# Query heads laid side by side by GpSimd ahead of the transposes, and a new order of loads, in a fused Sinkhorn-attention and token-mixing kernel

## The chip, the cores and the metric

The kernel runs on one core of a Trainium2 chip. The metric is the device time of one execution in microseconds (us). The kernel before takes 104.47 us (median of 4 runs, 104.46 to 104.66).

## What is computed

There are 4 batches with 8 heads, 768 positions and 64 columns per head; the positions form 8 blocks of 96.

```python
P = sort_net                                   # (4, 8, 8, 8)
for _ in range(5):                             # Sinkhorn
    P = exp(P - max(P, -1)); P /= sum(P, -1); P /= sum(P, -2)
k_s = einsum('bhij,bhjcd->bhicd', P, k_blocks); v_s = the same with v
attn = softmax(q_block @ k_s.T / 8) within each block
x = (attn @ v_s), heads side by side           # (4, 768, 512)
wq, wk = x @ w_q, x @ w_k                      # 64 columns each
out = relu((wq @ wk.T / 8) @ x) @ w_out        # (4, 768, 512), float32
```

The token mixing is reassociated: `wk.T @ x` is formed first (group G below), then multiplied by `wq`.

## The kernel before, in words

The whole program is written as one list of short items, `ORDER` (L18 to L42), and the loop at L479 issues them one by one. An item is a letter, a batch, a number and a last sign. Capital letters are groups of TensorE (PE) matmuls and the last sign is the PSUM bank; a small letter is the eviction of the group (q evicts Q, k evicts K, v evicts V, e is the exp of S, r and x evict P, and so on) and the last sign is the engine, A for ScalarE (ACT), D for VectorE (DVE), P for GpSimd (POOL), S for SyncE (SP). Each engine works through its items in the order of the list. Nothing is reordered later; waits come from the data and buffers that items share. `Q115` is thus the Q group of batch 1, number 1, into bank 5.

The groups on PE, for one batch:

- Q (L244, 3 groups): transposes of the query. The load leaves row p*6+r of a head in partition p, slot r. A group takes two slots r and four head pairs kp. For each it issues **two** transposes, one for each head (hh) of the pair: 64 columns of `Qn` as weights, the 128x128 identity `idb` as the moving operand, the result in one half of the 128 PSUM partitions. So a group has 16 matmuls and a batch 48. q evicts to `QT`.
- K (L266, 4 groups): the sorted key, with `M` (a Kronecker matrix of P, built by n, L223) as the moving operand; k evicts to `KT`. Each group writes two 64-partition halves.
- F and A for batch 0, V and the DMAs R (L316) for the others: the sorted value; it ends in `VT`.
- S (scores), P (attention times value, with a column for the sum), T (transposes of X), J (x times w_q and w_k), W, G, H and O (the last product, 4 matmuls of 512 columns each).
- Z: fillers at the start that compute nothing.

Tiles that matter here: `Qn`, `Kn`, `Vn` have three buffers each (L95, L96), one for a batch, and batch 3 goes into that of batch 0. `QT`, `KT`, `VT`, `E`, `X` have two. The first four heads of batch 0's query come by SP as float32 into a stage (L154) and are cast by ACT into `Qn` (items i04, i05, L185); the other four come with item l00.

All other loads are DMAs that POOL issues (u_l, L200): l*b*0 is the query of batch b, l*b*1 the key, l*b*2 the value, l03 w_q and w_k, l04 w_out. They convert from float32 to bfloat16 on their way and go through one queue (q0 in the profile). POOL's items in order:

```
l00 l01 l02 i00 i02 l03 l11 l10 l12 l04 n11 n10 l20 n21 n20
N11v l21 l30 N11v N10v N12v l22 l32 l31 n30 n31
```

The items N (u_N, L321) are **gates**: a copy of one element out of `Vs`, which POOL can only do once the eviction v of batch 1 with that number has written it. What stands behind a gate in POOL's list, such as the key of batch 2 (l21), is issued after it.

Of the kernel before, what the change touches and what calls it, by code (L numbers as in the profile page):

```python
# [9 lines left out]
BF16 = mybir.dt.bfloat16  # L10
# [5 lines left out]


ORDER = """  # L18
l00P l01P l02P i00P i02P l03P c00D c01D i01D Z080 l11P c02D i03A Z250 c03D Z350 i04A l10P c04D Z440
i05A Q027 c05D Q016 q02A Q005 Z540 q00A b00D l12P B004 Z020 q01A n01D n00D l04P K010 u00A n03D K002  # L20
n11P n02D k01A K036 k00D K024 k03A S020 n10P k02D S012 e02A S056 F034 e01A S000 f03D l20P e05A F022
A035 f02A S066 a03D e00A A024 F012 e06A a02D F000 f01A K136 n21P f00D P044 A013 r04D A002 k13D a01A
n20P K100 x04D S036 k10A a00D K114 e03A S040 k11D P002 e04A P016 r00D Q115 x00D r01D P020 x01D q11A
Q104 r02D P032 q10A x02D V116 T005 v11A N11v l21P l30P r03D Q124 x03D V100 t00A V126 q12A v10D T015
T033 T022 v12A N11v N10v N12v l22P t03D S110 l32P t02D t01A S123 V136 e11A J012 v13D J005 e12A J032
S150 R12S j01D J025 R15S e15A S106 j00D R10S Q214 R11S d01D l31P Q203 e10A R14S q21D R13S W002 Q225
q20D d00A S160 w00D W014 q22A K126 w01D G003 e16A n30P k12A G013 K230 g01D K224 n31P k23A S136 k22D
H002 e13A K200 h00D S244 k20A H026 h02A S200 K212 e20A k21D O057 e24A H010 o05D S212 O046 h01A S234
e21A O007 e23A O033 o00D o04A P140 S264 o03A y02S Q302 r14D e26A x14D P116 S144 r11D Q313 x11D e14A
P100 q30A P134 r10D x10D V206 q31A O022 r13D x13D v20A V230 T103 v23A P126 T135 t10A r12D V210 x12D  # L30
O014 o02A v21A y01S V222 t13D T117 o01D v22A T126 V330 t11D y00S V304 t12D R20S S252 v30A Q327 R21S
v33D R25S J106 e25A R24S q32D R22S J115 R23S J126 V310 j10A J135 S222 v31D j11A W104 V326 e22A d11S
W115 w10D K300 v32D d10A G104 k30A K322 R30S K336 R32S w11A S300 k32A R33S k33D G114 R31S e30A R35S
K312 g11D R34S S366 k31D S354 e36A H110 e35A H106 h11D S312 h10A S334 P210 e33A O107 r21D e31A x21D
P204 O116 o10A r20D x20D P230 o11A P222 r23D H124 y10S x23D T207 h12A O126 r22D x22D t20A P300 O145
o12A r30D x30D T214 o14A T227 P242 t21D S325 t22A S340 r24D O134 x24D e32A T237 e34A o13D P312 J205
t23A y11S r31D P330 x31D J214 J225 P326 r33D j20A x33D J234 T303 d20S j21A W202 O155 t30A r32D d21S
w20D x32D W212 G203 w21A o15D P340 T312 r34D G213 y12S x34D T327 t31D g21A T336 t32D H220 t33A H202
H214 h22D J307 J316 h21D J327 O251 j30A d30A W300 h20D J336 O247 w30A j31A o25D G300 d31A o24A W316
O221 y22S w31D G310 o22A O237 g31A H320 o23A H312 H304 h32A O206 y21S O217 o20A O351 o21A h30D h31A  # L40
O340 y20S o35A O307 o34D y38S O321 y37S o30A O310 y33S o32D O337 o31A y35S y34S o33B y36S
"""  # L42


# [1 line left out]
def kernel(  # L46
# [11 lines left out]
    nc = tc.nc  # L58
    B, H, S, D = q.shape
# [3 lines left out]
    P = 128  # L63
    R6 = S // P
    SP = BLK // R6
    NP = H // 2
# [16 lines left out]
    sb = ctx.enter_context(tc.tile_pool(name="sb", bufs=1))  # L83
    psp = ctx.enter_context(tc.tile_pool(name="psp", bufs=1, space=bass.MemoryType.PSUM))

    def tiles(name, n, shape, dtype=BF16):
        return [sb.tile(shape, dtype, name=f"{name}{i}") for i in range(n)]

    PS = psp.tile([P, 8, 512], FP32, name="ps")
    ENG = {"A": nc.scalar, "D": nc.vector, "P": nc.gpsimd, "S": nc.sync}  # L90
# [2 lines left out]
    nc.sync.dma_start(out=Pm[:, 0:NB, :], in_=sort_net.rearrange("b h i j -> (b h) i j"))  # L93

    NIN = 3  # L95
    Qn, Kn, Vn = (tiles(n, NIN, [P, H, R6, D]) for n in ("Qn", "Kn", "Vn"))  # L96
    wqk = sb.tile([P, PT, 2, DH], BF16, name="wqk")
    wo = sb.tile([P, PT, DM], BF16, name="wo")

    def load(t, src, b):  # L100
        nc.gpsimd.dma_start(out=t[b % NIN].rearrange("p h r d -> p h (r d)"),  # L101
                            in_=src[b].rearrange("h (p r) d -> p h (r d)", p=P))

    QT = tiles("QT", 2, [P, NP, R6, P])
# [20 lines left out]
    idb = sb.tile([P, P], BF16, name="idb")  # L125
# [13 lines left out]
    def mm(o, w, x, start=True, stop=True, t=False):  # L139
        nc.tensor.matmul(o, w, x, is_transpose=t, start=start, stop=stop, skip_group_check=True)  # L140

    def copy(e, o, i):
        if e == "A":
            nc.scalar.copy(o, i)  # L144
        else:
            nc.vector.tensor_copy(o, i)  # L146

    def bf(n):
        return PS[:, n, :].bitcast(BF16)
# [3 lines left out]
    stage = mixT[0].rearrange("p a c r s -> p (a c r s)").bitcast(FP32).rearrange("p (h e) -> p h e", h=HQ)  # L153
# [21 lines left out]
    def u_i(b, n, e):  # L175
        if n == 0:
            nc.gpsimd.memset(idb, 0.0)
            nc.gpsimd.affine_select(out=idb, in_=idb, compare_op=ALU.not_equal, fill=1.0, base=0,
                                    pattern=[[-1, P]], channel_multiplier=1)
        elif n == 1:  # L180
            nc.vector.reduce_max(m_p, idb.rearrange("p (j s) -> p s j", s=SP), axis=AX.X)
        elif n == 3:
            nc.scalar.copy(Lx.rearrange("p i j s -> p (i j) s"),
                           idb[0:BH, 0:BH].unsqueeze(2).to_broadcast([BH, BH, SP]))
        elif n in (4, 5):  # L185
            h = 2 * n - 8
            copy(e, Qn[0][:, h:h + 2].rearrange("p h r d -> p h (r d)"), stage[:, h:h + 2])
        elif n == 2:
            for t in VT:
                nc.gpsimd.memset(t.rearrange("p i (h e) -> p i h e", e=DS)[:, :, :, D:DS], 1.0)  # L190
            for t in Vs:
                nc.gpsimd.memset(t[:, :, :, D:DS], 1.0)
            for t in KT:
                nc.gpsimd.memset(t[:, :, S:S + P - BLK], 0.0)
            for t in E:
                nc.gpsimd.memset(t[:, :, 2 * TH * BLK:EW], 0.0)
                nc.gpsimd.memset(t[:, NT - 1, 2 * (NB * NP - TH * (NT - 1)) * BLK:EW], 0.0)  # L197


    def u_l(b, n, e):  # L200
        if n == 3:
            for s, w in enumerate((moe_w_q, moe_w_k)):
                nc.gpsimd.dma_start(out=wqk[:, :, s, :], in_=w.rearrange("(t p) d -> p t d", p=P))  # L203
        elif n == 4:
            nc.gpsimd.dma_start(out=wo, in_=moe_w_out.rearrange("(t p) d -> p t d", p=P))
        elif b == 0 and n == 0:
            nc.gpsimd.dma_start(out=Qn[0][:, HQ:H].rearrange("p h r d -> p h (r d)"),  # L207
                                in_=q[0, HQ:H].rearrange("h (p r) d -> p h (r d)", p=P))
        else:
            load((Qn, Kn, Vn)[n], (q, k, v)[n], b)  # L210
# [30 lines left out]
            mm(PS[:, bank, :], filw[:, b, :], fil)  # L241


    def u_Q(b, n, bank):  # L244
        ps = bf(bank).rearrange("p (k r s) -> p k r s", k=NP, r=2)
        for r in range(2):
            for kp in range(NP):
                for hh in range(2):
                    mm(ps[hh * D:(hh + 1) * D, kp, r, :], Qn[b % NIN][:, 2 * kp + hh, 2 * n + r, :],
                       idb, t=True)  # L250

    def u_q(b, n, e, bank):
        copy(e, QT[b % 2][:, :, 2 * n:2 * n + 2, :].rearrange("p k r s -> p k (r s)"),
# [225 lines left out]
    for item in ORDER.split():  # L479
        kind, b, n, arg = item[0], int(item[1]), int(item[2:-1]), item[-1]  # L480
# [40 lines left out]
```

## Time and profile before

| | |
|---|---|
| median of 4 runs | 104.47 us |
| the profiled execution | 104.42 us |
| its span in the profile | 102.3 us |
| TensorE clock granted | 0.996 of full |
| busy share | PE 89%, ACT 75%, DVE 70%, POOL 24% |
| first Q group begins | 9.55 us |
| last matmul ends | 98.4 us |
| bytes through the load queue | 9.70 MB |

The span begins with the first instruction of the profile, and all times below are from there. A line of the timeline gives start, duration, engine, source line, operation, the tiles written and read, and how many instructions were merged; a bracket tells the idle time ahead of it and what ended that. A matmul's own duration (some 220 ns) is a latency; groups of them are pipelined, so their pace is read from the starts of one group and of the next.

### The profile page before, as it was taken

How to read it: one execution, taken by the hardware profiler on the slowest of the kernel's cores; microseconds unless marked ns; L12 is line 12 of the kernel's file. 1: busy time of each engine (PE TensorE's matmuls, PEld its weight loads, DVE VectorE, ACT ScalarE, POOL GpSimd, SP SyncE). 2: the span in 40 equal slices, each digit the busy share in tenths (PEclk: the TensorE clock that was granted, in tenths of full speed). 3: DMA queues.
4: the chain of work that ended last, by engine and by line, in shares of the span. 5: the costliest groups of instructions: out<-in, count | busy, mean ns of one | idle time of the engine just before them, and what ended most of it. 6: DMA issues, size and time to landing. Idle time of an engine off the chain costs nothing.

```text
span 102.3 us, 3324 instructions
## 1 busy us (share of the span) xinstructions
PE 90.8 (89%) x1411; PEld 59.1 (58%) x1420; DVE 71.3 (70%) x135; ACT 76.4 (75%) x115; POOL 24.6 (24%) x41
## 2 busy tenths in 40 slices
PE   3997988889879998899999999789999999999940
PEld 1233566678657686545867668556778665444410
DVE  3876786589987874653898967779979999304420
ACT  5355979949859997999699789994896446678430
POOL 5999667540018954000000000000000000000000
PEclk9999999999999999999999999999999999999998
DMA  1899999999999999999999999652305150234992
GB/s 18 285 208 204 203 192 200 203 208 201 205 207 203 208 199 247 253 220 203 208 297 205 320 340 200 161 147 75 136 0 210 40 205 0 82 139 197 371 345 103
DMA packets 19133, 19.57 MB, mean 191 GB/s; under 512 B 1904, under 2 KB 17200, under 8 KB 19120
## 3 DMA queue, kind: packets, MB, share of 16 engines
q0 software_dynamic: 13552, 9.70, 62.3%
q1 hardware_dynamic: 5568, 9.67, 28.2%
q8 instruction: 11, 0.18, 0.7%
q14 instruction: 2, 0.02, 0.0%
HBM read 20.19 MB, written 6.29 MB: 259 GB/s over the span
## 4 chain that ended last, share of the span: by engine, by line
PE 47%; DMA 30%; POOL 9%; ACT 7%; issue 2%; DVE 2%; ACTq 0%; DVEq 0%; POOLq 0%
PE ps L140 47%; DMA Vn<-in_v_dram 18%; DMA Kn<-in_k_dram 9%; DMA qD<-qkT 3%; POOL Kn L101 2%; ACT E L347 2%; ACT KT L144 1%; POOL wqk L203 1%; DVE mixT L453 1%; POOL E L197 1%; ACT qkT L144 1%; ACT mixT L451 1%; POOL Qn L207 1%; POOL Vn L101 1%; POOL Qn L101 1%
## 5 line engine op out<-in xcount | busy, mean ns | idle before, releaser
L347 ACT ACTIVATE E<-ps 96x960 bf16<-96x960 f32 (+1 forms) x28 | 24.0, 913 | 0.9 <-PE ps L140 0.9
L140 PE MATMUL ps<-wo,mixT 128*128 128x512 bf16 x88 | 22.5, 380 | 0.5
L381 DVE TENSOR_TENSOR X<-ps,R 96x896 bf16<-96x896 f32 (+1 forms) x20 | 20.1, 1005 | 0.6
L140 PEld LDWEIGHTS <-mixT 128*128 128x128 bf16 x96 | 8.5, 97 | 9.3 <-issue 0.8
L144 ACT COPY ot<-ps 128x512 f32<-128x512 f32 (+1 forms) x16 | 9.2, 580 | 5.2 <-PE ps L140 5.2
L140 PE MATMUL ps<-VT,E 96*128 96x65 bf16 x256 | 11.0, 193 | 0.7 <-DVE mixT L453 0.7
L140 PEld LDWEIGHTS <-E 96*128 96x128 bf16 x256 | 9.7, 97 | 2.9 <-issue 0.9
L140 PE MATMUL ps<-fil,filw 128*128 128x512 bf16 x27 | 8.8, 475 | 2.4 <-DVE filw L161 1.6
L453 DVE TENSOR_SCALAR mixT<-ps 128x1024 bf16<-128x1024 f32 x6 | 7.2, 1219 | 5.0 <-PE ps L140 4.9
L146 DVE COPY ot<-ps 128x512 f32<-128x512 f32 (+1 forms) x9 | 5.9, 657 | 6.0 <-PE ps L140 4.6
L140 PE MATMUL ps<-QT,KT 64*128 64x96 bf16 x256 | 9.8, 204 | 0.3 <-ACT KT L144 0.3
L144 ACT COPY QT<-ps 128x1024 bf16<-128x1024 bf16 x9 | 8.8, 1016 | 0.7 <-PE ps L140 0.6
L146 DVE CAST KT<-ps 128x768 bf16<-128x768 f32 x8 | 7.5, 949 | 2.6 <-PE ps L140 2.6
L231 POOL TENSOR_TENSOR M<-PTR,m_p 128x512 bf16<-128x512 bf16 x6 | 7.8, 1313 | 4.8 <-PE ps L140 3.1
L140 PEld LDWEIGHTS <-KT 64*128 64x128 bf16 x256 | 6.6, 94 | 3.9 <-issue 1.5
L140 PE MATMUL ps<-M,Kn 128*64 128x128 bf16 x192 | 7.6, 221 | 1.4 <-DMA Kn<-in_k_dram 0.9
L140 PEld LDWEIGHTS <-Kn 128*64 128x64 bf16 x192 | 6.1, 109 | 3.2 <-DMA Kn<-in_k_dram 1.3
L140 PEld LDWEIGHTS <-X 96*128 96x128 bf16 x128 | 6.4, 98 | 1.6 <-issue 0.4
L140 PE MATMUL ps<-idb,X 96*128 96x96 bf16 x128 | 7.3, 206 | 0.0
L144 ACT CAST KT<-ps 128x768 bf16<-128x768 f32 x8 | 6.4, 799 | 1.0 <-PE ps L140 0.9
L140 PE MATMUL ps<-idb,Qn 128*64 128x128 bf16 x192 | 7.1, 221 | 0.0
L140 PEld LDWEIGHTS <-filw 128*128 128x128 bf16 x28 | 2.7, 115 | 7.2 <-ACT filw L166 2.3
(77 smaller groups left out, 137.9 us busy)
## 6 DMA issues: line engine op xcount, KB each, us to landing
out_dram<-ot SPq DMA_DIRECT2D x9, 512.0 KB, 3.9
Kn<-in_k_dram POOLq DMA_DIRECT2D x4, 768.0 KB, 10.7
Vn<-in_v_dram POOLq DMA_DIRECT2D x4, 768.0 KB, 17.4
VT<-Vs SPq DMA_DIRECT2D x18, 132.0 KB, 4.3
Qn<-in_q_dram POOLq DMA_DIRECT2D x3, 768.0 KB, 15.5
out_dram<-ot SPq DMA_DIRECT2D x6, 256.0 KB, 2.1
mixT<-in_q_dram SPq DMA_DIRECT2D x1, 768.0 KB, 4.5
wo<-in_moe_w_out_dram POOLq DMA_DIRECT2D x1, 512.0 KB, 20.1
```

The lines of the kernel that those rows point to most:

```text
L101: nc.gpsimd.dma_start(out=t[b % NIN].rearrange("p h r d -> p h (r d)"), in_=src[b].rearrange("h (p r) d -> p h (r d)", p=P))
L140: nc.tensor.matmul(o, w, x, is_transpose=t, start=start, stop=stop, skip_group_check=True)
L144: nc.scalar.copy(o, i)
L146: nc.vector.tensor_copy(o, i)
L197: nc.gpsimd.memset(t[:, NT - 1, 2 * (NB * NP - TH * (NT - 1)) * BLK:EW], 0.0)
L203: nc.gpsimd.dma_start(out=wqk[:, :, s, :], in_=w.rearrange("(t p) d -> p t d", p=P))
L207: nc.gpsimd.dma_start(out=Qn[0][:, HQ:H].rearrange("p h r d -> p h (r d)"), in_=q[0, HQ:H].rearrange("h (p r) d -> p h (r d)", p=P))
L231: ENG[e].tensor_tensor(out=M[b % 2][:, h0:h1], in0=src.unsqueeze(2).to_broadcast([P, nh, SP, NB]), in1=m_p.unsqueeze(1).unsqueeze(3).to_br ...
L347: nc.scalar.activation(E[b % 2][:, n, 0:2 * w * BLK].rearrange("p (t a c) -> p a t c", a=2, c=BLK), PS[0:BLK, bank:bank + 2, 0:w * BLK].re ...
L381: nc.vector.tensor_mul(xo.rearrange("p (a t d) -> p a t d", a=2, d=D), avps(bank, w)[:, :, :, 0:D], rr[b, n][:, :, 0:w].unsqueeze(3).to_br ...
L451: nc.scalar.activation(o, i, ACT.Relu)
L453: nc.vector.tensor_relu(o, i)
```

## The change

`Qn` gets two buffers instead of three, and a new tile `Qp` (one buffer for all batches) holds each head pair side by side: 128 columns for a slot r and a pair kp. A new item p (u_p) copies a pair from `Qn` to `Qp`; POOL does 14 of them (two for batch 0, four for each other batch). For batch 0's first four heads the casts i04 and i05 on ACT write into `Qp` directly. A Q group then has 8 transposes with 128 columns of weights, and a batch 24. The gates N are gone. `ORDER` is written anew: besides the new items many groups stand elsewhere, and 57 evictions change their engine (28 go to ACT, 28 to DVE, the copy d00 to SP).

```diff
-    Qn, Kn, Vn = (tiles(n, NIN, [P, H, R6, D]) for n in ("Qn", "Kn", "Vn"))
+    Kn, Vn = (tiles(n, NIN, [P, H, R6, D]) for n in ("Kn", "Vn"))
+    Qn = tiles("Qn", 2, [P, H, R6, D])
+    Qp = sb.tile([P, NP, R6, 2, D], BF16, name="Qp")
...
-            copy(e, Qn[0][:, h:h + 2].rearrange("p h r d -> p h (r d)"), stage[:, h:h + 2])
+            copy(e, Qp[:, n - 4].rearrange("p r h d -> p h r d"),
+                 stage[:, h:h + 2].rearrange("p h (r d) -> p h r d", d=D))
...
+    def u_p(b, n, e):
+        ENG[e].tensor_copy(Qp[:, n].rearrange("p r h d -> p h r d"), Qn[b % 2][:, 2 * n:2 * n + 2])
+
     def u_Q(b, n, bank):
         ps = bf(bank).rearrange("p (k r s) -> p k r s", k=NP, r=2)
         for r in range(2):
             for kp in range(NP):
-                for hh in range(2):
-                    mm(ps[hh * D:(hh + 1) * D, kp, r, :], Qn[b % NIN][:, 2 * kp + hh, 2 * n + r, :],
-                       idb, t=True)
+                mm(ps[:, kp, r, :], Qp[:, kp, 2 * n + r].rearrange("p h d -> p (h d)"), idb, t=True)
```

POOL's items in the new order:

```
l00 l01 l02 i00 i02 p02 p03 l03 l11 l10 n10 n11 l12 n20 n21 l20
p13 l04 p11 p10 p12 l21 p22 l32 p23 n31 p21 l30 p20 n30 l22 l31
p31 p33 p30 p32
```

PE's items around the first Q group of batch 1 and of batch 2 in the new order:

```
F022 A037 S030 K122 K134 A027 K110 P012 P004 S066 S040 P046 K102 P020 T005 P032
Q124 V136 V110 Q115 T014 Q107 T026 T033 V120 J002 V103 J022 J017 S160 S125 W002
J037 S133 S100 G002 W015 S146 S110 G012 S154 Q203 Q211 Q220 H002 H026 K224 K200
```

More of the change, by code (lines that the diff above doesn't have):

```diff
@@ L18 @@
 ORDER = """
[L19 to L38, printed above, removed]
@@ L39 @@
-H214 h22D J307 J316 h21D J327 O251 j30A d30A W300 h20D J336 O247 w30A j31A o25D G300 d31A o24A W316
-O221 y22S w31D G310 o22A O237 g31A H320 o23A H312 H304 h32A O206 y21S O217 o20A O351 o21A h30D h31A
-O340 y20S o35A O307 o34D y38S O321 y37S o30A O310 y33S o32D O337 o31A y35S y34S o33B y36S
+l00P l01P l02P i00P i02P c00D c01D i01D Z080 c02D i03A Z250 c03D Z350 i04A p02P p03P l03P c04D Z440
+i05A Q007 c05D Q016 q00A Q025 Z540 q02A b00D l11P B004 Z020 q01A n03D n02D K030 l10P u00A n00D K022
+n01D n10P k03A K006 k02D K014 k00A S050 k01D n11P F032 e05A F016 F004 f03A f01D S020 f00A S002 l12P
@@ new lines @@
+A017 e00A A006 a01D S014 e02A F022 a00D A037 n20P f02D e01A S030 a03D K122 n21P e03A l20P K134 k12D
+A027 k13A K110 a02D P012 k11A P004 r01D S066 x01D S040 e06A p13P e04A P046 r00D K102 x00D l04P p11P
+P020 k10A r04D p10P x04D T005 p12P r02D P032 x02D t00A Q124 V136 r03D q12D V110 v13A l21P Q115 x03D
+T014 v11A Q107 t01A T026 T033 t02D V120 q10A t03D J002 p22P v12D l32P q11A V103 J022 J017 v10D p23P
+j00A S160 S125 d00S W002 e16A n31P J037 R15S e12A S133 w00D R14S j01D S100 G002 R10S e10A R11S d01D
@@ new lines @@
+p21P W015 R12S S146 R13S w01D e13A S110 l30P p20P G012 e11A S154 n30P Q203 g01A Q211 e14A q20D Q220
+q21D H002 e15A H026 q22D h02A K224 h00D K200 k22A O057 k20A K232 o05A K214 k23D S200 k21A H016 h01D
+S262 e20A l22P S234 e23A S240 O017 e24A S214 o01D O026 e26A e21A V300 o02D P132 l31P v30A V314 r13D
+P126 x13D v31A S250 e25A P114 r12D x12D P102 O001 p31P r11D r10D S226 x11D O030 p33P e22A x10D T115
+p30P o03A P146 T124 t11A o00D y01S T100 p32P V332 t12D y00S O041 v33A r14D t10D V224 x14D o04A J110
@@ new lines @@
+v22D T137 y02S V212 t13A J101 v21D V234 J121 J130 v23A V206 j10D Q303 j11A d10D W101 Q312 v20A d11D
+w10D W110 K324 q31D q30A R24S K316 R20S w11D G101 k32D R23S k31A K332 R25S G111 R21S k33A K304 R22S
+V326 g11A k30D Q320 v32A H102 q32D H124 h10A H116 R34S h12D S360 R31S R33S e36A S312 R35S h11D S340
+R32S e31A O155 R30S e34A S332 P236 e33A O114 r23D x23D o15A P220 o11A O123 r22D x22D P214 o12A O132
+r21D x21D T223 o13A P200 t22A P246 y11S S354 r20D r24D O102 x20D e35A T213 x24D o10A T205 P340 t21D
@@ new lines @@
+y10S S326 t20A r34D T232 x34D e32A P333 J205 r33D t23A S300 x33D P326 e30A J225 J212 r32D x32D j20A
+P313 P300 d20A J232 r31D W205 r30D T337 j21A x31D T326 w20A d21S W212 t33A G205 x30D w21A T313 t32A
+G215 t31D T302 g21A O143 t30A H220 o14A H214 H206 h22A J302 h21D y12S J313 h20A J322 O241 j30D J333
+d30A W300 O222 o24A j31D w30D d31A W313 G307 o22A w31D O256 G317 o25A O235 g31D y22S H320 o23A H312
+H306 h32D O214 y21S O205 o21A O351 o20A h30D h31A O340 y20S o35A O307 o34D y38S O321 y37S o30D O310
@@ L42 @@
+y33S o32A O337 o31A y35S y34S o33B y36S
 """
@@ L100, in load @@
     def load(t, src, b):
-        nc.gpsimd.dma_start(out=t[b % NIN].rearrange("p h r d -> p h (r d)"),
+        nc.gpsimd.dma_start(out=t[b % len(t)].rearrange("p h r d -> p h (r d)"),
                             in_=src[b].rearrange("h (p r) d -> p h (r d)", p=P))
```

## The prediction

> **What bounds the kernel now.** I read the chain that ended last first, on the page and then in order of time. The page's shares:
>
> ```profile
> PE 47%; DMA 30%; POOL 9%; ACT 7%; issue 2%; DVE 2%; ACTq 0%; DVEq 0%; POOLq 0%
> ```
>
> PE carries the end and loads carry the front. In order of time the chain has two long transfers (columns: start, duration, what):
>
> ```profile
> 10.32 18.44 DMA Vn<-in_v_dram
> ...
> 30.20 0.18 POOL gate L333
> ...
> 30.44 8.86 DMA Kn<-in_k_dram
> ```
>
> The value of batch 1 lands at 28.75 us, the key of batch 2 at 39.3. The timeline of PE shows what they hold up:
>
> ```profile
> 21.60 1.07 PE L140 MATMUL ps<-idb,XT 128*96 128x128 bf16 x16
> ...
> 25.98 0.61 PE L140 MATMUL ps<-VT,E 96*128 96x65 bf16 x14
> 26.52 0.64 PE L140 MATMUL ps<-idb,Qn 128*64 128x128 bf16 x16
> ...
> 28.80 0.50 PE L140 MATMUL ps<-Vn,M 128*128 128x384 bf16 x2 [1.10 <-DMA Vn<-in_v_dram]
> ...
> 35.20 1.08 PE L140 MATMUL ps<-idb,Qn 128*64 128x128 bf16 x32
> ...
> 39.34 0.86 PE L140 MATMUL ps<-M,Kn 128*64 128x128 bf16 x24 [0.26 <-DMA Kn<-in_k_dram]
> ...
> 65.19 0.37 PE L140 MATMUL ps<-qD,Ab 64*128 64x512 bf16 x1 [0.36 <-DMA qD<-qkT]
> ...
> 66.95 0.59 PE L140 MATMUL ps<-VT,E 96*128 96x65 bf16 x14 [0.75 <-DVE mixT L453]
> ...
> 78.15 0.60 PE L140 MATMUL ps<-VT,E 96*128 96x65 bf16 x14
> 78.59 0.33 PE L140 MATMUL ps<-XT,wqk 128*128 128x384 bf16 x1
> ...
> 91.27 7.08 PE L140 MATMUL ps<-wo,mixT 128*128 128x512 bf16 x31
> ```
>
> The waits are short; the rest is PE at its pace. From the starts of such lines each kind of group has a price in us: O 0.86, V 0.33, J 0.16 per matmul, P 0.44 (0.25 for the short one), Q 0.45, A 0.45, T 0.34, K and F 0.34, S 0.21, G 0.44, H 0.22, W 0.22, a filler 0.22. A further 0.095 us falls due where PE goes between whole-array matmuls and ones that use a half of its rows or columns: the 14 P matmuls take 0.54 us up to a Q group (25.98 to 26.52) and 0.44 up to a J (78.15 to 78.59). All groups of the list together are 76.7 us, with 77 such changes 84.0. The last matmul ends at 98.35 (91.27 + 7.08), so some 14.3 us are waits, 4.7 of them ahead of the first Q group at 9.55.
>
> **The transposes themselves: nothing saved but 13 changes, 1.24 us.** The line at 35.20 has 32 half-width transposes with starts spread over 0.86 us (1.08 less a latency of 0.22). They run in pairs, the two halves of the array at once: 16 pairs, 57 ns for a pair. The line at 21.60 has 16 transposes that use the whole height and also 128 moving columns: (1.07 - 0.22) / 15 = 57 ns for one. A new transpose replaces a pair at the same pace. What goes are changes of the array's mode around Q: the new list has 64, so it sums to 76.7 + 64 x 0.095 = 82.8. Bounds for this: 0 if the changes are merely shifted, 1.24 if all show. [...]
>
> **The loads: no gain from the missing gates.** The gate at 30.20 kept POOL waiting for 8.5 us, yet the load queue had work all that time. Three issues, by tile (w_out at 11.18, then the queries of batch 1 at 9.45 and batch 2 at 16.24), tell it:
>
> ```profile
> DMA to landing us min/median/max: 20.1/20.1/20.1
> ```
> ```profile
> DMA to landing us min/median/max: 15.5/15.5/15.5
> ```
> ```profile
> DMA to landing us min/median/max: 18.9/18.9/18.9
> ```
>
> So they land at 31.3, 25.0 and 35.2, in order of issue, and the key of batch 2, held back by the gate, at 39.3, 4.1 us behind the one ahead of it, the usual step of 3.8 to 4.2. The queue is bound by its rate. The new order has the same bytes ahead of the first query (25.0), the first value (28.75) and the key of batch 2 (39.3); only query 2 passes w_out: 28.75 + 3.85 = 32.6. If its first loads came too late to keep the queue full, the price would be the gap; the key of batch 1 is issued some 3 us later than before (behind two copies), at about 11.3 us, while value 0 fills the queue until 15.3. I take 0.
>
> **The copies by POOL: a new wait.** Before, a query landed and PE transposed it 0.4 us later (25.0, 25.4). Now four copies stand in between, in POOL's order, with other work among them. The trace shows no such copy (128 partitions x 768 elements). The nearest rows of POOL's timeline:
>
> ```profile
> 6.53 0.60 POOL L197 MEMSET E<- 96x608 bf16 x1
> ...
> 17.91 1.29 POOL L231 TENSOR_TENSOR M<-PTR,m_p 128x512 bf16<-128x512 bf16 x1 [0.71 <-PE ps L140]
> ```
>
> The memset, which reads nothing, gives 0.60 x 768 / 608 = 0.76 us; the product of two inputs gives 1.3 x 768 / 512 = 1.95. A copy reads one input, without the product's broadcast patterns, so I take 0.95, nearer to the memset, and keep both ends. [...]
>
> Batch 0: p02 and p03 start at 7.6 (its load lands 6.3 us after 1.25) and end at 9.5. Q starts at 9.55 now. Nothing lost, but every 0.1 above 0.95 would cost 0.2, which the fillers Z540 cover up to some 0.8.
>
> Batch 1: POOL waits at p13 until 25.0. Behind it stand the issue of w_out (0.81), p11, p10, p12, the key of batch 2. p12 ends at 25.0 + 4 x 0.95 + 0.81 = 29.6. PE gets to Q124 earlier: the key of batch 1 lands at 20.8, from K122 to Q124 are 5.1 us of groups, and this stage lost 0.5 to waits before; 26.4 to 26.9. So it idles some 3 us. [...]
>
> Batch 2: the query lands at 32.6. In POOL's order then come p22, a load (0.87), p23, M (1.31), p21, a load (0.88), p20, 4 x 0.95 + 3.06 = 6.9 us: p20 ends at 39.5. PE gets to Q203 at 29.6 + 8.5 of groups + 0.5 to 1 of waits = 38.6 to 39.1, and waits again. Batch 3's copies have PE's work of 18 us from Q203 to Q303 as cover, of which 10 remain after its query's landing near 49.4; they cost nothing unless one takes above 2 us.
>
> **The sum.** At 39.5 the new kernel stands before Q203. Ahead of it are 24.76 us of groups and 28 changes, so 82.8 - 27.4 = 55.4 us are left. Before, at 39.34 (the key of batch 2) 54.9 us were left and the end came at 98.35: 98.35 - 39.34 - 54.9 = 4.1 us of waits in the rest. With the same waits the new end is 39.5 + 55.4 + 4.1 = 99.0, 0.65 later. The tail behind the last matmul is the same list of evictions and stores, 3.9 us. The profiled execution took 104.42 (2.1 outside its span; the median of the runs is 104.47), so 105.1. What the 1.24 us give is spent, because PE's arrivals at Q124 and Q203 are set by POOL. The 57 evictions on another engine go both ways (28 and 28) and I set them at 0, with 1 us to either side: the waits of 0.36 and 0.75 at 65 and 67 us could go (d10 and d11 are now DVE copies instead of a DMA), others could come, since ACT is busy for 4 to 5 of each 5 us from 30 to 65.
>
> **Rivals.**
>
> 1. *Faster.* A copy takes 0.76 and the two waits at 65 and 67 us vanish. p20 ends at 32.6 + 3.04 + 3.06 = 38.7; 38.7 + 55.4 + 3.1 = 97.2, so 103.3; with only one of these, 104.0 to 104.3. It decides from copies under 0.8 us. For it: the memset's row; against: a copy also reads. 0.27.
> 2. *No change.* The transposes keep their pace, the queue keeps its order, and the copies' wait just eats the mode changes: the change doesn't do what it says. 104.3 to 104.6; 0.10.
> 3. *Much slower.* A copy is like the product: at 1.4 us Q124 comes at 31.5 and p20 ends at 32.6 + 5.6 + 3.06 = 41.3, the end 2.45 later, 106.9. At 1.95 p22 itself is late (34.6, behind p12 and the key's issue): 34.6 + 7.8 + 3.06 = 45.5 and 111. For it: the only computing row of POOL at this size; against: two inputs. 0.18.
>
> The forecast, gated by copies of 0.85 to 1.2 us: 104.7 to 106.3; 0.45.
>
> **How the numbers follow.** The likeliest case gives 105.1. The range takes in the first rival but for its lowest part (0.1 is left below) and the third up to copies of 1.45 us (0.1 left above): 103.6 to 107.2. Faster or slower by 0.2%, about what a measurement of this kernel can tell from no change, is 0.2 us: faster 0.27, same 0.10, slower 0.63.
>
> **What would show it.** Right: a copy of 0.85 to 1.2 us; PE idle for 2 to 4 us ahead of Q124 with POOL as the releaser and Q124 at 29 to 30.5; Q203 at 39 to 40.5, released by POOL; transposes 56 to 58 ns apart; landings at 25, 28.8, 32.6 and 39.3. Wrong: copies under 0.75 us; a query that lands earlier than 24; waits behind 40 us that sum to under 3 or over 5.5; transposes far from 57 ns; a granted clock below 1.00 behind 26 us.

## The result, and the profile after

The changed kernel takes 104.66 us (median of 54 runs), the kernel before 104.44 us (median of 78 runs beside them). The ratio is 1.0038 with a 95% interval of 1.0025 to 1.0052: slower by 0.4%. Of the 54 runs, 44 lie at 104.45 to 105.03 us and ten at 105.57 to 106.31 (medians here are of all runs, ratios leave out runs over 1.5% above their kernel's fastest). The profiled execution took 105.87 us (span 104.0), and TensorE's clock stood at half for 3.41 us in it; its other steps are read below, and for the end a profile without this (experiment `e2_wout_behind`, nearly the same kernel) stands beside it.

The page's shares of the chain that ended last, of the changed kernel:

```profile
PE 55%; DMA 13%; DVE 9%; ACT 8%; POOL 7%; issue 3%; POOLq 0%; ACTq 0%
```

DMA had 30% before and has 13% now, POOL's share went from 9 to 7. In order of time the same chain (start, duration, what):

```profile
21.11 11.65 DMA Qn<-in_q_dram
...
32.91 0.83 POOL Qp L249
33.74 0.81 POOL Vn L104
34.55 0.83 POOL Qp L249
35.38 1.26 POOL M L235
36.64 0.80 POOL Qp L249
37.44 0.89 POOL Qn L104
38.33 0.85 POOL Qp L249
39.23 3.38 PE ps L143 x29
```

Where the key of batch 2 held the end up to 39.3 before, the query of batch 2 and all of POOL's list behind it do so now. A copy takes 0.80 to 0.85 us of this chain (0.82 to 0.87 by its own record, which overlaps the next one's). The four copies are half of the 6.3 us from the first to the end of the last; the rest are two issues of loads and a product M. PE's timeline shows both waits for copies (the bracket is the idle time ahead and what ended it):

```profile
27.90 0.28 PE L143 MATMUL ps<-idb,Qp 128*128 128x128 bf16 x2
28.66 0.51 PE L143 MATMUL ps<-idb,Qp 128*128 128x128 bf16 x6 [0.48 <-POOL Qp L249]
29.01 0.81 PE L143 MATMUL ps<-Vn,M 128*128 128x384 bf16 x4
...
37.14 0.63 PE L143 MATMUL ps<-X,wk 96*64 96x256 bf16 x8 [0.52 <-DVE wk L149]
37.70 0.39 PE L143 MATMUL ps<-QT,KT 64*128 64x96 bf16 x10
39.23 2.39 PE L143 MATMUL ps<-idb,Qp 128*128 128x128 bf16 x24 [1.14 <-POOL Qp L249]
...
92.57 7.08 PE L143 MATMUL ps<-wo,mixT 128*128 128x512 bf16 x32
```

The 24 transposes at 39.23 take 2.39 us here. In `e2_wout_behind`, after the same wait but at full clock, they take 1.51, so (1.51 - 0.22) / 23 = 56 ns for one:

```profile
39.44 1.51 PE L143 MATMUL ps<-idb,Qp 128*128 128x128 bf16 x24 [1.14 <-POOL Qp L249]
```

A Q group ahead of a whole-array group, first in the kernel before, then in the changed one, took 0.57 us up to the next group's start and takes 0.45:

```profile
57.46 0.64 PE L140 MATMUL ps<-idb,Qn 128*64 128x128 bf16 x16
58.03 1.31 PE L140 MATMUL ps<-XT,wqk 128*128 128x384 bf16 x7
```
```profile
60.78 0.61 PE L143 MATMUL ps<-idb,Qp 128*128 128x128 bf16 x8
61.23 0.39 PE L143 MATMUL ps<-idb,qkT 128*96 128x128 bf16 x4
```

The loads, by tile as before (w_out, the query of batch 1, the query of batch 2):

```profile
DMA to landing us min/median/max: 9.6/9.6/9.6
```
```profile
DMA to landing us min/median/max: 13.0/13.0/13.0
```
```profile
DMA to landing us min/median/max: 11.7/11.7/11.7
```

With the issues at 25.50, 11.65 and 21.11 they land at 35.1, 24.7 and 32.8; the first value of batch 1 lands at 28.6 and the key of batch 2 at 39.2.

### The profile page after: what moved, and what is told of

Same layout as the page of the kernel before. It is cut to its first block, busy times and chain, and to the rows that moved or that the text cites. A ratio compares the mean times of both kernels' runs of the same rounds, so it can differ in the third digit from the quotient of the medians.

```text
span 104.0 us, 3144 instructions
## 1 busy us (share of the span) xinstructions
PE 90.1 (87%) x1315; PEld 59.4 (57%) x1324; DVE 71.7 (69%) x136; ACT 76.2 (73%) x115; POOL 34.7 (33%) x51
## 3 DMA queue, kind: packets, MB, share of 16 engines
q1 hardware_dynamic: 5488, 9.62, 26.9%
## 4 chain that ended last, share of the span: by engine, by line
PE 55%; DMA 13%; DVE 9%; ACT 8%; POOL 7%; issue 3%; POOLq 0%; ACTq 0%
PE ps L143 55%; DMA Qn<-in_q_dram 11%; POOL Qp L249 3%; POOL M L235 2%; ACT Vs L147 2%; ACT mixT L456 2%; DMA Pm<-in_sort_net_dram 2%; DVE tmp L173 1%; DVE Pm L175 1%; DVE M L235 1%; DVE Pm L172 1%; DVE tmp L170 1%; ACT Pm L168 1%; DVE tmp L171 1%; DVE tmp L174 1%
## 5 line engine op out<-in xcount | busy, mean ns | idle before, releaser
L249 POOL COPY Qp<-Qn 128x768 bf16<-128x768 bf16 x14 | 11.3, 830 | 14.3 <-DMA Qn<-in_q_dram 14.3
L147 ACT COPY ot<-ps 128x512 f32<-128x512 f32 (+1 forms) x19 | 10.9, 578 | 6.9 <-PE ps L143 6.7
L458 DVE TENSOR_SCALAR mixT<-ps 128x1024 bf16<-128x1024 f32 x7 | 8.5, 1222 | 3.5 <-ACT ot L147 1.9
L147 ACT COPY XT<-ps 128x768 bf16<-128x768 bf16 x10 | 8.1, 805 | 1.8 <-PE ps L143 1.6
L143 PE MATMUL ps<-idb,Qp 128*128 128x128 bf16 x96 | 7.7, 236 | 1.7 <-POOL Qp L249 1.6
L147 ACT CAST KT<-ps 128x768 bf16<-128x768 f32 x10 | 7.9, 800 | 0.8 <-PE ps L143 0.6
L143 PEld LDWEIGHTS <-Qp 128*128 128x128 bf16 x96 | 6.6, 106 | 2.8 <-POOL Qp L249 2.2
L147 ACT CAST Vs<-ps 128x768 bf16<-128x768 f32 x8 | 6.3, 805 | 2.2 <-PE ps L143 1.7
L149 DVE CAST KT<-ps 128x768 bf16<-128x768 f32 x6 | 5.6, 952 | 3.1 <-PE ps L143 2.9
```

The source lines that it names most:

```text
L249: ENG[e].tensor_copy(Qp[:, n].rearrange("p r h d -> p h r d"), Qn[b % 2][:, 2 * n:2 * n + 2])
L458: nc.vector.tensor_relu(o, i)
```

## The experiments

Times are medians; the kernel before ran beside each set and lay at 104.4 to 104.8. The "last matmul" is the start of the last one in a kernel's profile: 97.97 us in the kernel before, 99.27 in the changed one, 98.16 in `e2_wout_behind`.

**1. The order alone, no copies.** The changed order and engines, but the old half-width transposes straight from `Qn`, and no items p:

```diff
-                mm(ps[:, kp, r, :], Qp[:, kp, 2 * n + r].rearrange("p h d -> p (h d)"), idb, t=True)
+                for hh in range(2):
+                    mm(ps[hh * D:(hh + 1) * D, kp, r, :], Qn[b % 2][:, 2 * kp + hh, 2 * n + r, :],
+                       idb, t=True)
```

> The changed kernel's order, loads and evictions, but without the copies: the query is transposed from Qn by pairs of half-width transposes as before, ACT casts batch 0's heads into Qn. Theory: PE pays the 13 changes of mode again (1.24 us), the waits of 0.8 to 1.1 at Q124 and 1.14 at Q203 go, V136 is held by value 1 at 28.6: 104.1 to 104.6, about the kernel before. Rival (the time went into the order of the other groups and their evictions, not into the copies): no wait to win, 1.24 to pay, 105.5 to 105.9.

Measured: 103.60 us, ratio 0.9923 (0.9909 to 0.9937). The direction is that of the theory, the gain is larger. The last matmul is at 97.53 with all of the 84.0 us of work, 0.44 earlier than before, and the tail behind it is shorter by 0.2. So the rest of the new order is worth some 0.4 to 0.8 us by itself.

**2. Where that gain comes from.** First the kernel before with one letter changed: the copy d11 of the queries' second chunk goes to DVE, as in the changed order, in place of a DMA.

```diff
-... e22A d11S W115 w10D ...
+... e22A d11D W115 w10D ...
```

> The kernel before with one eviction moved: the second chunk of batch 1's qD (d11) is copied by DVE and not sent by a DMA. Theory (a part of the changed order's own gain of some 0.65 us of waits, seen without copies, comes from this): the waits of 0.36 to 0.5 ahead of H106 and of 0.75 to 0.86 ahead of P210 at 65 to 67 us shrink, 103.4 to 104.1 us. Rival (the gain is spread over the whole order, the waits there have other causes): 104.3 to 104.6.

Measured: 103.78 us, ratio 0.9931 (0.9908 to 0.9954), all four runs at 103.68 to 103.94. The theory holds. Its PE timeline, to be read against the lines at 65.19 and 66.95 of before:

```profile
64.41 0.39 PE L140 MATMUL ps<-qD,Ab 64*128 64x512 bf16 x1
...
66.31 0.59 PE L140 MATMUL ps<-VT,E 96*128 96x65 bf16 x14 [0.23 <-DVE mixT L453]
```

The wait for `qD` (0.36) is gone and that for `mixT` fell from 0.75 to 0.23. Then the reverse: experiment 1 with d11 as a DMA again.

```diff
-... j11A d10D W101 Q312 v20A d11D w10D ...
+... j11A d10D W101 Q312 v20A d11S w10D ...
```

> The changed order with the old half-width transposes and no copies, as measured at 103.60, but with the second chunk of batch 1's qD (d11) sent by a DMA again, as before. Theory (the order's own gain of 0.85 is that one eviction): the waits ahead of H106 and P210 or of what stands there now come back, 104.2 to 104.6 us. Rival (the other 56 moved evictions share in it): 103.6 to 104.0.

Measured: 103.79 us, ratio 0.9906 (0.9879 to 0.9933), the last matmul at 97.24. This time the rival holds: the gain stays without the copy on DVE. SP's queue offers a reason, first in the kernel before, then in this one:

```profile
57.01 4.54 SPq L317 DMA_DIRECT2D VT<-Vs  x6
61.65 0.56 SPq L406 DMA_DIRECT2D qD<-qkT  x1
```
```profile
58.85 0.50 SPq L411 DMA_DIRECT2D qD<-qkT  x1
59.56 7.84 SPq L322 DMA_DIRECT2D VT<-Vs  x11
```

Before, the DMA stands behind six transfers of `VT` and lands at 65.15, as the line at 65.19 waits. In the new order it stands ahead of them and lands at 61.4, and H102 reads the chunk at 63.4. So it seems that there are two ways to lose the same wait, another engine for the copy or another place in SP's list, and that the changed order has both and gains once; the place in SP's list was not tried by itself on the kernel before.

**3. The gates alone.** The kernel before without the four items N.

```diff
-... T005 v11A N11v l21P l30P ... q12A v10D T015 T033 T022 v12A N11v N10v N12v l22P ...
+... T005 v11A l21P l30P ... q12A v10D T015 T033 T022 v12A l22P ...
```

> The kernel before, with the items N11v, N11v, N10v, N12v taken out and nothing else. Theory (the load queue is bound by its rate and first come, first served): the key of batch 2 is issued some 8 us earlier and lands at 39.3 as before, value 1 at 28.8, so 104.2 to 104.6, no change. Rival (the gates keep later loads from taking a share of the rate): value 1 lands later than 29.5 and the end comes 0.5 to 2 us later. Second rival (the gates cost time): key 2 lands before 38 and the end is 0.4 or more earlier.

Measured: 104.55 us, ratio 1.0016 (0.9999 to 1.0032). The key of batch 2 is issued at 21.66 and not at 30.44, and its answer of the trace says how long it then lies in the queue:

```profile
DMA to landing us min/median/max: 17.6/17.6/17.6
```

It lands at 39.3 as ever. Issued 8.8 us earlier, this load waits 8.7 us longer (17.6 and 8.9 us to landing); the gates cost nothing.

**4. The order of POOL's list around the copies.** First w_out's load behind batch 1's copies:

```diff
- p13 l04 p11 p10 p12 l21 p22
+ p13 p11 p10 p12 l04 l21 p22
```

> The changed kernel, with the load of w_out (l04) behind batch 1's four copies instead of among them. Theory: p12 ends 0.75 us earlier, Q124 comes at 27.9, but the value of batch 1 lands at 28.6, so V136 gains at most 0.4; and Q203 still waits for p20 at 39.2, which hangs on the landing of query 2 at 32.8. So nothing at the end: 104.5 to 104.7. Rival (the first wait, at Q124, is what costs): 0.5 to 0.8 less, 103.9 to 104.2.

Measured: 104.93 us, ratio 1.0054 (1.0023 to 1.0085). That is 0.2 above the theory's range and far from the rival's. Batch 1's queries are ready 0.3 us earlier (28.3), the V group behind them starts at 29.01 in both kernels, and Q203 still waits for POOL until 39.44: nothing is gained at the end, as the theory says. Then batch 2's copies together, and the loads behind them:

```diff
- l21 p22 l32 p23 n31 p21 l30 p20 n30
+ l21 p22 p23 p21 p20 l32 n31 l30 n30
```

> The changed kernel, with batch 2's four copies (p22, p23, p21, p20) issued by POOL directly one behind the other, and the two loads and two builds of M that stood among them behind them. Theory (POOL's copies set when PE gets to Q203): p20 ends at 32.8 + 4 x 0.80 = 36.0 instead of 39.2, PE reaches Q203 by its own at 38.1 and doesn't wait; the wait of 1.14 us goes, so 103.5 to 103.9 us against 104.66, and the clock doesn't fall behind 38 us. Rival (ACT's evictions set the pace from 30 to 50 us, and the wait for the copy only stands in front of them): 104.4 to 104.7, the wait comes back at K224, O057 or S240 with ACT as the releaser.

Measured: 102.95, 103.20, 105.73 and 106.60 us; the ratio, from the first two, is 0.9871 (0.9849 to 0.9894), a larger gain than the theory's. With so few runs it was run again.

> The changed kernel with batch 2's four copies together behind batch 1's key work, the loads behind them, once more and in five rounds, since the first time left few comparable runs. Theory (Q203's wait of about a microsecond is gone and the clock keeps its full speed, as Q203 no longer idles): 102.9 to 103.3 us. Rival (the first runs were lucky): 103.4 to 103.9.

Measured: 103.06, 103.30, 103.73, 104.94, 105.86 and 106.84 us; the ratio, from the first three, is 0.9893 (0.9851 to 0.9935). The first half of the theory holds: the wait ahead of Q203 is gone. The second half is open: the two traced executions of this kernel (103.20 and 103.30 us) keep the full clock up to the last matmul, the other eight were not traced. POOL's and PE's timeline of this kernel:

```profile
33.14 3.13 POOL L249 COPY Qp<-Qn 128x768 bf16<-128x768 bf16 x4 [3.55 <-DMA Qn<-in_q_dram]
36.21 0.87 POOL L104 DMA_DIRECT2D Vn<-in_v_dram  x1
```
```profile
37.63 1.52 PE L143 MATMUL ps<-idb,Qp 128*128 128x128 bf16 x24
```

The last copy ends at 36.3 where it ended at 39.2, and Q203 starts at 37.63 without a wait. The copies, one behind the other, come every 0.77 us ((3.13 - 0.83) / 3). The last matmul is at 96.66, 1.50 ahead of `e2_wout_behind`. Putting three other items behind the copies is worth more than the whole change cost. Both moves together:

> Both moves together: w_out behind batch 1's copies, batch 2's copies directly one behind the other. Theory: both waits gone, PE held by the landing of value 1 (28.6) alone; 1.14 from Q203 and 0.3 to 0.4 from Q124: 103.1 to 103.6. Rival (ACT sets the pace): 104.3 to 104.6, the same as with the second move alone.

Measured: 103.15 us, ratio 0.9874 (0.9857 to 0.9891). That is within the theory's range. The next thing is late at once, which the theory doesn't have:

```profile
40.44 0.86 PE L143 MATMUL ps<-M,Kn 128*64 128x128 bf16 x24 [1.04 <-DMA Kn<-in_k_dram]
```

The key lands at 40.39, 5.0 us behind w_out (35.35); in the changed kernel it was 4.2 (39.24 and 35.08). w_out's later issue doesn't explain it: in `e1b_copies2_first_again`, where that load stands where it did, the key lands at 40.42. In both, transfers through q1 (of `VT` and `qD`) move more beside the key (0.48 and 0.45 MB from 35.3 to 40.5 us) than in the changed kernel (0.27) and in `e1_copies2_first` (0.37), where the key lands at 39.24; this fits, but was not tried.

The last step was that key's load ahead of w_out's:

```diff
- p12 l04 ... l21 p22 p23 p21 p20
+ p12 l21 l04 ... p22 p23 p21 p20
```

> The kernel with batch 1's and batch 2's copies each kept together (measured 103.15, with a wait of 1.0 for the key of batch 2 at 40.4), with the load of that key issued ahead of w_out's. Theory (the queue is first come, first served: the key takes w_out's place and lands near 37, w_out, needed at 41, near 39.5): the wait of 1.0 goes, 102.0 to 102.6 us. Rival (something else is late behind it: w_out itself, or the evictions of that stage): 102.8 to 103.3.

Measured: 104.16 us, ratio 0.9938 (0.9894 to 0.9981), outside of both. The key of batch 2 does land at 36.5, its wait is gone, and P114 comes at 49.03 (49.49 in `e3_both`). Then the key of batch 3 is late:

```profile
60.49 0.86 PE L143 MATMUL ps<-M,Kn 128*64 128x128 bf16 x24 [1.52 <-DMA Kn<-in_k_dram]
```

It was the last in the load queue; the one ahead of it landed at 53.9. In the changed kernel it needs 3.9 us from there (53.4 to 57.2), here 6.6 (53.89 to 60.45). The table of queues for these stretches (packets, MB, the time that their packets took), first the changed kernel, then this one:

```profile
q0 software_dynamic: 760, 0.57, 94.8%
q1 hardware_dynamic: 26, 0.11, 6.8%
```
```profile
q1 hardware_dynamic: 450, 1.57, 60.0%
q0 software_dynamic: 674, 0.51, 50.0%
```

The stores of the first batch's output go through q1. PE is ahead here, so SP issues them from 52.87 and not from 56.19, and they fall on the last load. In `e1_copies2_first` and `e3_both`, whose stores go out at 53.4 and 53.3, the same load takes 4.9 and 5.4 us. So a faster front seems to start a transfer that the back then waits for; holding the stores back was not tried.

**5. Each copy twice.** The rise with the copies' duration:

```diff
-        ENG[e].tensor_copy(Qp[:, n].rearrange("p r h d -> p h r d"), Qn[b % 2][:, 2 * n:2 * n + 2])
+        for _ in range(2):
+            ENG[e].tensor_copy(Qp[:, n].rearrange("p r h d -> p h r d"), Qn[b % 2][:, 2 * n:2 * n + 2])
```

> The changed kernel, with each copy p done twice by POOL (the same bytes again), all else the same. Theory (PE's arrivals at Q124 and Q203 hang on POOL's copies): p12 ends near 32.5 instead of 28.6, p20 near 42.9 instead of 39.2, Q203 comes 3.7 us later and so does the end: 107.8 to 108.8 us, or another 1.2 if the clock falls in the longer wait. Rival (the copies stand beside ACT's work and the wait has little weight): under 106.5.

Measured: 112.53 us, ratio 1.0775 (1.0729 to 1.0821): right in direction, too low in size, even with the clock's fall. p12 ends at 32.4, 3.7 us later, as expected; Q203 starts at 46.7, 7.5 later and not 3.7. Two things come on top:

```profile
36.88 1.72 POOL L250 COPY Qp<-Qn 128x768 bf16<-128x768 bf16 x2 [3.69 <-PE ps L143]
```

`Qp` has one buffer, so batch 2's first copy waits until PE has read batch 1's last pair: it starts 3.1 us after its query's landing (33.75), while in the other kernels with the changed order it starts 0.15 us after. And PE read that pair late because the copies ended late and because its clock stood at half from 30.35 to 37.18; it did so again from 47.42 to 50.83.

**6. The old order with the copies.** The kernel before, gates and all, with copies and whole-height transposes; the copies stand together ahead of their batch's first Q group.

```diff
- ... r00D Q115 x00D ... S106 j00D R10S Q214 ... o03A y02S Q302 ...
+ ... r00D p10P p11P p12P p13P Q115 x00D ... R10S p20P p21P p22P p23P Q214 ... y02S p30P p31P p32P p33P Q302 ...
```

> The order of before, gates and all, with the copies put in: p02 and p03 ahead of l03, and four copies each right ahead of Q115, Q214 and Q302 in the list; full-width transposes; two buffers for Qn. Theory (a copy stands between a landing and a transpose that waits for it): Q115 moves from 25.4 to 28.4 and Q214 from 35.2 to 39.5, because query 2 lands at 35.2 behind w_out and POOL comes to it behind the gates; 106.5 to 108.5 us. Rival (only the 13 changes of mode matter, the copies hide): 103.0 to 103.6.

Measured: 108.05 us, ratio 1.033 (1.0279 to 1.0381), as the theory has it. PE goes to Q115 at once and then takes one matmul for each copy:

```profile
25.84 0.23 PE L143 MATMUL ps<-idb,Qp 128*128 128x128 bf16 x1 [0.17 <-POOL Qp L249]
26.60 0.23 PE L143 MATMUL ps<-idb,Qp 128*128 128x128 bf16 x1 [0.54 <-POOL Qp L249]
27.37 0.23 PE L143 MATMUL ps<-idb,Qp 128*128 128x128 bf16 x1 [0.54 <-POOL Qp L249]
28.14 0.45 PE L143 MATMUL ps<-idb,Qp 128*128 128x128 bf16 x5 [0.54 <-POOL Qp L249]
```

The clock then stands at half from 29.01 to 32.42. The new order of groups puts K, P and T work in front of Q124, where PE waits 0.48 us for POOL; in the old order it waits four times, 1.8 us in all. The two kernels also differ in the loads' order and in the gates, so how much of the 3.4 us between them is the groups' order is not shown.

**7. No copies for batch 0.** Experiment `e1_copies2_first`, with all of batch 0's query transposed from `Qn` in halves, as before, and no p02 and p03.

> The first experiment's kernel (batch 2's copies one behind the other), and batch 0's query transposed straight from Qn by half-width pairs, without p02 and p03. While these two copies run, one DVE product of the Sinkhorn chain takes 0.70 instead of 0.21 us and all of PE's start is 0.45 later; that goes here. Theory: K122 waits for the key of batch 1 (lands at 20.8 to 21.0) in both, so the end stays within 0.2 of the first experiment's, 102.9 to 103.4. Rival (the start's delay reaches the end): 102.5 to 102.8.

Measured: 103.61 us, ratio 0.9922 (0.9901 to 0.9944): neither. The front is 0.2 to 0.3 earlier up to B004, as the rival has it. At K122 the lead is gone, since this group waits for the key of batch 1, which lands at 20.96. Batch 1's queries then come 0.15 later, and at 41 us the difference is 0.5:

```profile
41.79 1.04 PE L143 MATMUL ps<-wo,mixT 128*128 128x512 bf16 x3 [0.61 <-ACT mixT L459]
```

Why that chain over `qD`'s DMA (landing at 39.66, 38.97 in `e1_copies2_first`) is longer is not settled; in two executions of the kernel of `e1_copies2_first` itself this landing differs by 0.38 (38.97 and 39.35).

## Why the prediction came out as it did

The forecast was 0.65 us slower through a wait for POOL; it is 0.2 by the medians and 0.4 by the ratio. The wait at Q203 is the predicted one, the wait at Q124 is a sixth of what was predicted, and sizes are off in both directions. The sum, in starts of the last matmul: 97.97 before; the 13 changes of the array's mode take 1.24 off by the prediction's price, an estimate that was not measured apart; the order takes 0.44 off (experiment 1); the copies add what is left up to the 98.16 of `e2_wout_behind`, 97.97 - 1.24 - 0.44 + 1.87. Experiment 4 shows that most of this 1.87 is no price of copying: with the copies together the last matmul is at 96.61 and 96.66, so 0.3 to 0.4 remain.

- **Transposes: right.** 56 ns for one, as for a pair before. Ahead of a whole-array group a Q group takes 0.45 us where it took 0.57, so the change of mode there is gone (0.12 for this one, 0.095 in the sum).
- **Loads and gates: right.** Landings at 24.7, 28.6, 32.8 and 39.2 against 25.0, 28.75, 32.6 and 39.3; experiment 3 shows that the gates were free.
- **A copy: 0.80 to 0.85 us, not 0.95.** One behind the other they come every 0.77. The row of the memset was the right one to be near to, and nearer than taken.
- **Batch 1: the step that failed most.** "It idles some 3 us": PE waited 0.48 for POOL within Q124, and at most 0.3 more ahead of it. POOL was early (p12 ends at 28.6, not 29.6: 0.7 from the copies, 0.3 from an earlier landing). And PE was late: Q124 starts at 27.9, not at 26.4 to 26.9, as this stage lost 1.8 us to waits, not 0.5, among them 0.36 ahead of P046 for ACT's exp and 0.52 within T005. The end did not feel it, which is luck for the forecast: as experiment 4's first part shows, Q203 waits for POOL anyway.
- **Batch 2: right.** Q203 at 39.2 and 39.4, predicted 39.5, released by POOL, after 6.3 us of POOL's list (6.9 predicted). Part of this closeness is luck: the list was 0.6 shorter, the query landed 0.2 to 0.4 later.
- **Waits behind it: 3.7 us, not 4.1.** 98.54 (the end of the last matmul in `e2_wout_behind`) - 39.44 - 55.4 = 3.7. The 57 moved evictions were set at 0 with 1 us to either side; moving d11 alone shrank the waits at 65 and 67 us (experiment 2). The prediction says that d10 and d11 both were a DMA; only d11 was, d10 was a copy by ACT.
- **The tail: "the same list, 3.9 us", with 2.1 outside the span, was short by 0.2.** From the last matmul's end to the end of the execution `e2_wout_behind` takes 104.76 - 98.54 = 6.2 us. What is longer is told in the last section.
- **The clock: not in the sum, and it does fall.** In the profiled execution it fell at Q203, and the last matmul came 1.1 us later than in `e2_wout_behind` (99.27 and 98.16). A granted clock below 1.00 behind 26 us was one of the prediction's signs of being wrong, and it came. How often it fell in the executions that were not traced is open: a mean clock of 0.972 to 0.984 stands beside times of 104.5 and of 105.9.
- **Batch 0: "nothing lost" holds at the end only.** Here a DVE operation took 0.70 us for 0.21 beside the copies (last section), and PE was 0.4 to 0.5 us later from Z440 on; the landing of the key of batch 1 at 20.8 hides it.

## What to carry to other kernels

Price work that is put on a helper engine by everything that its queue holds between the data's landing and the last piece, not by the piece: here four copies of 0.83 us became 6.3 us, and moving three items behind them was worth 1.5 us. Cycles taken from an engine whose arrival is set elsewhere came back here only when that other wait was cleared (ratios of 0.987 and 0.989 without the wait at Q203), and each one cleared showed the next (the queries, then the key of batch 2, then the key of batch 3, which earlier stores seem to delay). A new order can hold a gain that has nothing to do with its purpose: try its pieces alone on the old kernel, where one letter gave 0.7 us.

## What the runs showed of the hardware

**The granted clock stood at half behind stretches of 3.41 us in which PE was busy for 1.75 us or less.** The changed kernel's profile records the clock at full for 34.13 us, at half for 3.41 and at full for 61.44: ten times, once and 18 times 3.413. The kernel before has it at full for 95.57 us, 28 times that; `e7_old_order_copies` has 3.41 us at half, `e6_copies_twice` 6.83 and 3.41. In the changed kernel it fell at 39.64. Windows of its profile (length, then PE, PEld, DVE, ACT, POOL busy with counts, the clock, DMA share, GB/s):

```profile
39.00:40.00 1.00, 0.77 (x11) 0.78 (x12) 0.00 (x0) 0.91 (x2) 1.00 (x2) 0.82 1.24 244
40.00:41.00 1.00, 1.00 (x13) 1.00 (x11) 0.82 (x2) 0.00 (x0) 1.00 (x2) 0.50 1.22 249
...
43.00:44.00 1.00, 0.62 (x20) 0.45 (x16) 0.52 (x1) 0.98 (x2) 0.00 (x0) 0.97 1.22 252
```

The stretch ahead of the fall, and one of `e9_batch0_direct`, the emptiest of all after which there was no fall:

```profile
36.23:39.64 3.41, 1.75 (x44) 1.26 (x39) 0.82 (x2) 3.41 (x5) 3.41 (x5) 1.00 1.29 218
```
```profile
26.73:30.15 3.41, 1.93 (x32) 1.38 (x29) 2.32 (x5) 1.04 (x2) 3.08 (x4) 1.00 1.31 204
```

Over the fourteen profiles of the case, each divided into stretches of 3.413 us from the start of its record on, between the first 5 us and the last matmul, the clock fell after stretches with 0.67, 1.12, 1.63 and 1.75 us of PE's busy time, stayed at half after one with 1.74, and never fell after one with 1.93 or more. Where a wait lies counted here: `e2_wout_behind` has the same wait of 1.14 us, split over stretches with 2.56 and 2.40 us of busy time, and kept its clock. The runs don't show why the clock falls, nor what happens between 1.75 and 1.93 us.

**Some DVE operations took longer beside POOL's: 0.70 us for 0.21, and 1.40 for 0.25.** The same operation and shape, in the kernel before and in the changed one, first in the Sinkhorn steps, then the copy `qD`:

```profile
7.94 0.21 DVE L172 TENSOR_TENSOR Pm<-Pm,tmp 32x64 f32<-32x64 f32 x1
...
35.63 0.25 DVE L146 COPY qD<-qkT 64x384 bf16<-64x384 bf16 x1
```
```profile
7.93 0.70 DVE L175 TENSOR_TENSOR Pm<-Pm,tmp 32x64 f32<-32x64 f32 x1
...
35.37 1.40 DVE L149 COPY qD<-qkT 64x384 bf16<-64x384 bf16 x1
```

In the changed kernel POOL copies from 7.74 to 8.56 beside the first and forms the product M from 35.33 to 36.64 beside the second. The first `qD` copy of a profile takes 0.25 us in the four in which no copy or product of POOL is under way at its start or one ends within 0.1 us. In the ten others it ends 0.11 to 0.13 us after one of these does (in `e1_copies2_first` 36.13 after a copy's end at 36.02, in `e10_no_copies_d11_dma` 36.10 after a product's at 35.98; 0.23 in `e7_old_order_copies`, where it takes 2.21 us and lets two copies pass). The eviction of `qkT` from PSUM just ahead takes 0.54 to 0.56 us with copies and without. So the long ones went with POOL's work; what holds them up, the runs don't show. Here it cost 0.5 us ahead of a G group (the 0.52 at 37.14), which the wait at Q203 covered.

**The end of the program.** In the six profiles of kernels whose POOL list has the changed kernel's items, 69 instructions in the trace, POOL's very last instruction comes 0.43 to 0.45 us after the one ahead of it; in the eight others, with 54 to 83, it is 0.08. From the last eviction to the end of the execution these six take 5.34 to 5.39 us, the others 4.94 to 5.31. That goes with the tail's 0.2 us. No transfer of data lies in this gap in the changed kernel, and what it is was not tried.
